# Attention scores from 64-row products of even and odd heads, in place of one product with a block-diagonal key operand

## The chip, the cores and the metric

The kernel runs on one NeuronCore of a Trainium2 chip. The metric is the device time of one execution in microseconds (us). TensorE (PE) multiplies, with its weight loads (PEld) listed apart; VectorE (DVE), ScalarE (ACT) and GpSimd (POOL) do the rest, and SyncE (SP) issues the DMAs. The kernel before takes 1671.57 us, the median of three runs from 1668.79 to 1672.21.

## The reference, cut to what matters

Attention over keys and values that are averaged in groups of 8, and then two feed-forward layers on its 4608 rows of 512. There are 8 batches of 8 heads, 576 queries, 72 pooled keys and 64 numbers per head.

```python
k_p = k.reshape(B, H, Sp, pool, D).mean(axis=3)
v_p = v.reshape(B, H, Sp, pool, D).mean(axis=3)
scores = scale * np.matmul(q, k_p.transpose(0, 1, 3, 2))
attn = np.exp(scores - scores.max(-1)); attn = attn / attn.sum(-1)
x = np.matmul(attn, v_p)               # then per token, heads side by side
h = x @ w_in;   x = (h * np.cos(h)) @ w_out
h = x @ w_in2;  out = (h * np.clip(h + 3, 0, 6) / 6) @ w_out2
```

The change touches `scores` alone.

## The kernel before, in words

**Attention.** Each batch is cut into five units of queries (`UNITS`): four of 128 and one of 64, so 40 units, 32 full and 8 short. A unit's queries lie as `qT[n]`, 128 rows by 4 pairs of heads by up to 128 queries: rows 0 to 63 hold the even head of a pair, rows 64 to 127 the odd one. The pooled keys of a batch (`kbd`) are a block-diagonal operand, 128 rows by 4 pairs by 144 columns: the even head's 72 keys stand in rows 0 to 63 of the first 72 columns, the odd head's in rows 64 to 127 of the other 72, and the rest is zero from two memsets at the start (line 718). One matmul of a pair, with `qT` as the stationary operand and `kbd` as the moving one, so gives the scores of both heads beside each other (line 515). Everything here is fp32.

`unit_s(n, half)` makes two such matmuls, pairs 0 and 1 or pairs 2 and 3, into one PSUM tile of 288 columns. DVE then takes the maxima (line 525) and subtracts them on the way to SBUF (line 528); for batch 0 ACT does the exponentials straight from PSUM (line 535). `unit_exp`, `unit_norm`, `unit_pt` (transposes on PE, lines 586 and 610) and `pv` (products with the values, line 628; for the first four batches the second product of each pair has 64 rows) follow. The transposes of a short unit have 64 rows as well.

The keys are pooled in three ways. For batch 0, DVE halves the raw keys and ACT writes `kbd` in two pieces (line 434). For batch 1, PE sums them against an identity matrix (line 440) and ACT writes two pieces (line 445). For batches 2 to 7, DVE does all of it, the last addition in two pieces of 64 rows (line 432).

**Order.** `front()` runs batch 0 alone, while the first weights arrive and are converted. From then on the attention is a generator that is advanced piece by piece between the feed-forward's matmuls (line 299, first product; line 341, second): after each gemm step so many pieces are taken that a goal is met (lines 940 to 950), and each `yield` in `attention()` ends a piece. In this mixed stretch all small pieces share two PSUM tiles (`ap_ps`); in `front()` scores take turns between an `ap_ps` and an `h` tile. The order in which instructions stand on each engine in the built program is then set by a scheduler, which may move a matmul back or forth among the others as its operands and tiles come free; PE itself runs its queue in order.

After the attention the rest of the feed-forward runs: gemm matmuls at lines 299, 341 and 998, nearly without pause.

Of the kernel before, what the change touches and what calls it, by code (L numbers as in the profile page):

```python
# [8 lines left out]
F32 = mybir.dt.float32  # L9
# [4 lines left out]
AF = mybir.ActivationFunctionType  # L14
ALU = mybir.AluOpType
# [14 lines left out]
def tile_kernel(ctx, tc, q, k, v, wi1, wo1, wi2, wo2, ident_d, mask_d, out):  # L30
    nc = tc.nc
    B, H, S, D = v.shape
    DM, NT = out.shape
    P = 128
    N = 512
    SP = S // POOL
    NP = H // 2
# [30 lines left out]
    UNITS = [(n0, min(P, S - n0)) for n0 in range(0, S, P)]  # L68
    NU = len(UNITS)
# [292 lines left out]
    ap = actx.enter_context(tc.tile_pool(name="ap", bufs=1))  # L362
# [4 lines left out]
    vm = {}  # L367
    vr = {"vrf": ap.tile([P, NP, 2, D], F32, tag="vrh", name="vrf")}
    raw, kp = {}, {}
    kbd = [ap.tile([P, NP, 2 * SP], F32, name=f"kbd{n}") for n in range(2)]  # L370
    NE = 4
    ebuf = [ap.tile([P, H * SP + P], F32, name=f"e{n}") for n in range(NE)]
    raw_k = ap.tile([P, POOL * NP * SP], F32, name="raw_k")
    raw_t = ap.tile([P, KC, POOL * D], F32, name="raw_v")
    qm, qT, pts = {}, {}, {}
# [6 lines left out]
    sums = {}  # L382
    FACTOR = 1.0 / (math.sqrt(D) * POOL)

    def piece(kind):
        turn = turns[kind] = turns.get(kind, -1) + 1
        if started:
            return ps_a.tile([P, N], F32, tag="ap", name="ap_ps", bufs=2)
        tag = SKIND[kind][turn % len(SKIND[kind])]
        if tag == "ap":  # L390
            return ps_a.tile([P, N], F32, tag="ap", name="ap_ps", bufs=2)
        if tag == "h":
            return ps_h.tile([P, N], F32, tag="h", name="h")
        return ps_y.tile([P, N], F32, tag=tag, name=tag)

    def load_kv(b, nm, step=POOL):
        if nm == "v":
            src = v[b].rearrange("h (s r) d -> (h s) (r d)", r=POOL)
            pairs = src.rearrange("(j x) e -> x j e", x=2 * SP)
            nc.sync.dma_start(out=raw_t[:, :NP, :], in_=pairs[:P])  # L400
            for half in range(2):
                o = half * NP * VR
                nc.sync.dma_start(
                    out=raw_t[o : o + NP * VR, NP, :],
                    in_=src.rearrange("(j x) e -> j x e", x=2 * SP)[:, P:],
                )
            return
        for c in range(0, POOL, step):
            cs = slice(c * NP * SP, (c + step) * NP * SP)
            nc.sync.dma_start(out=raw_k[:, cs], in_=k[b][:, cs])  # L410

    def load_q(n):
        b, i = divmod(n, NU)
        n0, w = UNITS[i]
        t = ap.tile([P, NP, P], F32, tag="qT", name="qT", bufs=4)
        nc.sync.dma_start(
            out=t[:, :, :w], in_=q[b, :, :, n0 : n0 + w].rearrange("j p n -> p j n")
        )
        qT[n] = t

    def pool_k(b, eng):
        t = raw_k
        w = POOL * NP * SP
        while w > (2 if b else 1) * NP * SP:
            w //= 2
            eng.tensor_tensor(out=t[:, :w], in0=t[:, :w], in1=t[:, w : 2 * w], op=ALU.add)
        t = t[:, : 2 * NP * SP].rearrange("p (r j x) -> p r j x", j=NP, x=SP)
        kb = kbd[b % 2]
        for e, p in enumerate((slice(0, D), slice(D, P))):
            to = kb[p, :, e * SP : (e + 1) * SP]  # L430
            if b:
                eng.tensor_tensor(out=to, in0=t[p, 0], in1=t[p, 1], op=ALU.add)
            else:
                nc.scalar.activation(out=to, in_=t[p, 0], func=AF.Copy, scale=FACTOR)

    def sum_k(b):

        ps = piece("k")[:, : NP * SP]
        for c in range(POOL):
            nc.tensor.matmul(  # L440
                ps, ident, raw_k[:, c * NP * SP : (c + 1) * NP * SP],
                start=(c == 0), stop=(c == POOL - 1),
            )
        for e, p in enumerate((slice(0, D), slice(D, P))):
            nc.scalar.activation(
                out=kbd[b % 2][p, :, e * SP : (e + 1) * SP],
                in_=ps[p].rearrange("p (j x) -> p j x", x=SP), func=AF.Copy, scale=FACTOR,
            )

    def sum_v(b):  # L450
        ps = piece("w")[:, : KC * D].rearrange("p (c d) -> p c d", d=D)
        for r in range(POOL):
            nc.tensor.matmul(
                ps, ident, raw_t[:, :, r * D : (r + 1) * D], start=(r == 0), stop=(r == POOL - 1)
            )
        kp[b, "v"] = ps
# [12 lines left out]
    def make_v(b):  # L469
# [27 lines left out]
        for x, src, rows in (("h", f(sp_h), P), ("l", sp_l, half)):  # L497
# [8 lines left out]
                op=ALU.mult,  # L506
            )

    def unit_s(n, half):
        b, i = divmod(n, NU)  # L510
        w = UNITS[i][1]
        ps = piece("s")
        t = qT[n]
        for j in range(2):
            nc.tensor.matmul(  # L515
                ps[:w, j * 2 * SP : (j + 1) * 2 * SP],
                t[:, 2 * half + j, :w],
                kbd[b % 2][:, 2 * half + j, :],
                start=True,
                stop=True,  # L520
            )
        s3 = ps[:w, : 4 * SP].rearrange("p (g s) -> p g s", s=SP)
        mx = ap.tile([P, 4, 8], F32, tag="mx", name="mx", bufs=2)[:, :, 0:1]
        early = b < EARLY
        nc.vector.tensor_reduce(out=mx[:w, :, 0], in_=s3, op=ALU.max, axis=AX.X, negate=early)  # L525
        e = ebuf[n % NE][:w, half * 4 * SP : (half + 1) * 4 * SP].rearrange("p (g s) -> p g s", s=SP)
        if not early:
            nc.vector.tensor_tensor(
                out=e, in0=s3, in1=mx[:w].to_broadcast([w, 4, SP]), op=ALU.subtract
            )  # L530
            return
        if half == 0:
            sums[n] = ap.tile([P, H, 4], F32, tag="sm", name="sm", bufs=3)[:, :, 0:1]
        for g in range(4):
            nc.scalar.activation(
                out=e[:, g], in_=s3[:, g], func=AF.Exp, bias=mx[:w, g], scale=1.0,
                accum_out=sums[n][:w, 4 * half + g],
            )

    def unit_exp(n):  # L540
# [164 lines left out]
    def front():  # L705

        load_kv(0, "k")
        w_fetch()
        load_q(0)
        nc.sync.dma_start(out=ident, in_=ident_d)  # L710
        load_q(1)
        load_kv(0, "v")
        nc.sync.dma_start(out=mask[:, : 2 + NP], in_=mask_d)
        load_q(2)
        load_q(3)
        w_fetch()
        for n in range(2):
            nc.vector.memset(kbd[n], 0.0)
        nc.gpsimd.memset(vr["vrf"], 0.0)
        pool_k(0, nc.vector)  # L720
        w_convert(3)

        def s(n):
            unit_s(n, 0)
            unit_s(n, 1)

        s(0)
        load_q(4)
        s(1)
        unit_norm(0)  # L730
        w_convert(1)
        s(2)
        unit_norm(1)
        sum_v(0)
        unit_pt(0)
        s(3)
        make_v(0)
        load_kv(1, "k")
        w_ops(1)
        unit_pt(1)  # L740
        unit_pt_rest(0, 0)
        unit_norm(2)
        s(4)
        for j in range(NP):
            pv(0, 0, j)
        unit_norm(3)
        unit_pt(2)
        w_ops(1)
        unit_norm(4)
        unit_pt(3)  # L750
        unit_pt_rest(0, 2)
        unit_pt(4)
        (sum_k(1) if SUMMED > 1 else pool_k(1, nc.vector))
        load_kv(1, "v")
        load_q(5)
        load_q(6)
        load_q(7)
        w_convert(3)
        for j in range(NP):
            pv(0, 1, j)  # L760
        done.append(0)
        started.append(0)

    steps = []
    for bl in range(NB):
        n = NAL[bl]
        steps += [(0, (0, bl), bl, fc, fc == 0, fc == n - 1) for fc in range(n)]
    SA = len(steps)
    for bl in range(NB):
        n = NAL[bl]  # L770
# [10 lines left out]
    def w_fetch():  # L781
        nonlocal fetched
        if fetched < len(wjobs) and fetched < converted + 2:
            fetch_weights(*wjobs[fetched][:3])
            fetched += 1
# [4 lines left out]
    def w_ops(n):  # L790
        while running and n:
            running.pop(0)()
            n -= 1
            if not running:
                whole.add(wjobs[converted - 1][:3])
                w_fetch()
# [9 lines left out]
    def w_convert(n=3):  # L806
        nonlocal converted
        m, fc, hf, home = wjobs[converted]
        converted += 1
        running.extend(convert_weights(m, fc, hf))  # L810
        w_ops(n)
# [83 lines left out]
    for slot in range(2 * (T + LAG) + 4):  # L895
        s, odd = divmod(slot, 2)
        for fn in after.pop(slot, ()):
            fn()
        if not odd and s < T:
# [9 lines left out]
            if key[0] == 1 and fc == NF - 5:  # L909
                for c in range(NC):  # L910
                    t = ypl.tile([P, N], F32, tag="yv", name="yv", bufs=4)
                    nc.sync.dma_start(
                        out=t, in_=yp_d[c * P : (c + 1) * P, bl * N : (bl + 1) * N]
# [25 lines left out]
        if live:  # L939
            key = steps[s][1]  # L940
            i = sum(1 for x in steps[:s] if x[1] == key)
# [163 lines left out]
    for pb, (t0, w) in enumerate(PAIRS):  # L1105
# [3 lines left out]
        for g in range(4):  # L1109
# [17 lines left out]
            for n in range(7):  # L1127
# [4 lines left out]
                x = EARLY.get((g, n)) if pb == 0 else n if g == 3 else None  # L1132
# [15 lines left out]
    for step, pb in enumerate(ORDER2):  # L1148
        t0, w = PAIRS[pb]
# [75 lines left out]
```

## Time and profile before

| | |
|---|---|
| median of 3 runs | 1671.57 us |
| profiled execution | 1672.67 us |
| its span | 1670.9 us |
| PE / PEld busy | 1639.7 / 1348.0 us |
| DVE / ACT / POOL busy | 1108.9 / 891.6 / 311.9 us |

The profile is of one execution. Its span is counted from the first to the last instruction; what lies around it makes the execution's own time 1.8 us longer. A fp32 matmul appears in it as two matmul instructions with two weight loads; fp32r (the gemms) as one of each. Records of PE overlap, since a matmul's fill and drain run beside its neighbours, so the pace of PE is read from the distance between starts and not from the durations.

### The profile page before, as it was taken

Reading aid. Unit: us, or ns where it says so; the run is one execution under the profiler, and the core shown is the slowest. Engines: PE = TensorE matmul, PEld = TensorE weight load, DVE = VectorE, ACT = ScalarE, POOL = GpSimd, SP = SyncE. Lnnn points to the kernel's source line nnn. Section 1 sums busy time; section 2 is a strip of 40 time slices with the busy share of each in tenths; the row PEclk is TensorE's granted clock in tenths of the full one; section 3 lists DMA queues with packets and bytes.
Section 4 is the critical chain, followed back from the end, with each engine's and each line's share of the span. In section 5 each row is a group of like instructions: output and inputs, shape, how many; then the busy total and the mean of one; then the engine's idle time right before and its main releaser. Section 6 shows DMA issues by size and latency. Waiting matters only on the chain.

```text
span 1670.9 us, 21107 instructions
## 1 busy us (share of the span) xinstructions
PE 1639.7 (98%) x7674; PEld 1348.0 (81%) x7674; DVE 1108.9 (66%) x1536; ACT 891.6 (53%) x1320; POOL 311.9 (19%) x248
## 2 busy tenths in 40 slices
PE   6999999999999999999999999999999999999999
PEld 4656778888888888888888898888878888888889
DVE  5798666665767788878786445445364676768665
ACT  6667677776556554555555334444353444444444
POOL 3365343322223110111114001020120000000000
PEclk8999999999999999999999999999999999999999
DMA  7665351223333476666664483242439954335130
GB/s 241 205 217 195 115 182 51 92 89 124 114 114 119 143 246 198 209 213 202 187 189 154 152 290 141 111 164 114 177 130 336 341 185 168 130 123 170 58 118 34
DMA packets 154183, 273.03 MB, mean 163 GB/s; under 512 B 15712, under 2 KB 79328, under 8 KB 153056
## 3 DMA queue, kind: packets, MB, share of 16 engines
q1 hardware_dynamic: 154080, 271.70, 48.0%
q8 instruction: 60, 0.98, 0.2%
q14 instruction: 43, 0.35, 0.1%
HBM read 166.79 MB, written 104.86 MB: 163 GB/s over the span
## 4 chain that ended last, share of the span: by engine, by line
PE 93%; DVE 3%; DMA 2%; ACT 1%; issue 1%; POOL 1%; SPq 0%; POOLq 0%; DVEq 0%; ACTq 0%
PE bank L998 41%; PE h L299 22%; PE y L341 22%; PE ap_ps L628 3%; PE ap_ps L515 2%; PE ap_ps L586 1%; PE y L628 1%; DMA xr<-x_d 0%; DMA qT<-in_q_dram 0%; DMA st<-in_moe_w_out_dram 0%; POOL xl L277 0%; DVE a L132 0%; DVE mx L525 0%; PE y L440 0%; POOL e L557 0%
## 5 line engine op out<-in xcount | busy, mean ns | idle before, releaser
L998 PE MATMUL bank<-wa,wb 128*128 128x512 f32 (+1 forms) x1368 | 287.7, 358 | 0.0
L998 PEld LDWEIGHTS bank<-wa,wb 128*128 128x128 f32 x1368 | 231.2, 189 | 37.7
L299 PE MATMUL h<-xh,wb 128*128 128x512 f32 x648 | 211.2, 389 | 0.0
L341 PE MATMUL y<-gh,wb 128*128 128x512 f32 x648 | 210.8, 389 | 0.0
L860 ACT ACTIVATE wa<-wu 128x1024 fp32r<-128x1024 f32 (+1 forms) x130 | 127.3, 980 | 141.5 <-PE bank L998 121.4
L998 PE MATMUL bank<-wu,wb 128*128 128x512 f32 (+1 forms) x792 | 198.4, 386 | 0.0
L299 PE MATMUL h<-xh,wa 128*128 128x512 f32 x504 | 172.8, 402 | 2.5 <-ACT xh L276 2.5
L998 PEld LDWEIGHTS bank<-wu,wb 128*128 128x128 f32 x792 | 148.8, 188 | 29.9
L311 DVE SCALAR_TENSOR_TENSOR g<-h,t 128x512 f32<-128x512 f32 x144 | 99.0, 687 | 108.5 <-ACT t L306 108.1
L341 PE MATMUL y<-gh,wa 128*128 128x512 f32 x504 | 170.9, 399 | 0.0
L277 POOL TENSOR_TENSOR xl<-xr,xh 128x512 fp32r<-128x512 f32 x68 | 94.2, 1402 | 323.8 <-ACT xh L276 322.3
L306 ACT ACTIVATE t<-h 128x512 int32<-128x512 f32 x144 | 85.3, 592 | 124.3 <-PE h L299 123.8
L314 ACT ACTIVATE g<-g,bias_c 128x512 f32<-128x512 f32 x144 | 104.3, 724 | 79.7 <-DVE g L311 78.9
L299 PEld LDWEIGHTS h<-xh,wb 128*128 128x128 f32 x648 | 121.7, 188 | 25.2
L341 PEld LDWEIGHTS y<-gh,wb 128*128 128x128 f32 x648 | 121.6, 188 | 25.2
L321 ACT ACTIVATE gh<-g 128x512 fp32r<-128x512 f32 x144 | 90.4, 628 | 71.9 <-DVE g L318 71.6
L861 DVE TENSOR_TENSOR wa<-wu,wa 128x1024 fp32r<-128x1024 f32 (+1 forms) x80 | 89.4, 1122 | 57.2 <-ACT wa L860 57.1
L299 PE MATMUL h<-xl,wb 128*128 128x512 f32 x324 | 126.2, 389 | 0.0
L341 PE MATMUL y<-gl,wb 128*128 128x512 f32 x324 | 126.1, 389 | 0.0
L318 DVE TENSOR_TENSOR g<-h,g 128x512 f32<-128x512 f32 x144 | 98.6, 684 | 32.4 <-ACT g L314 31.6
L998 PE MATMUL bank<-wa,wa 128*128 128x512 f32 (+1 forms) x552 | 117.4, 359 | 0.0
L299 PEld LDWEIGHTS h<-xh,wa 128*128 128x128 f32 x504 | 94.6, 189 | 23.9 <-ACT xh L276 2.8
(177 smaller groups left out, 2854.9 us busy)
## 6 DMA issues: line engine op xcount, KB each, us to landing
g_d<-wu SPq DMA_DIRECT2D x64, 512.0 KB
wu<-g_d SPq DMA_DIRECT2D x56, 512.0 KB
wb<-s_d SPq DMA_DIRECT2D x36, 512.0 KB
xr<-x_d SPq DMA_DIRECT2D x68, 256.0 KB
s_d<-wa SPq DMA_DIRECT2D x32, 512.0 KB
s_d<-wa SPq DMA_DIRECT2D x32, 384.0 KB
raw_k<-in_k_dram SPq DMA_DIRECT2D x8, 1152.0 KB
yp_d<-ys SPq DMA_DIRECT2D x36, 256.0 KB
```

Source lines behind the costliest of these rows:

```text
L277: nc.gpsimd.tensor_tensor(out=xl, in0=t, in1=f(xh), op=ALU.subtract)
L299: nc.tensor.matmul(h, a[:, cs], z, start=(n == 0), stop=(n == 3 * NC - 1))
L306: nc.scalar.activation(out=t, in_=hs[s], func=AF.Copy, bias=0.25, scale=INV_2PI)
L311: mark[s] = nc.vector.scalar_tensor_tensor(out=g, in0=hs[s], scalar=INV_2PI, in1=t, op0=ALU.mult, op1=ALU.subtract)
L314: nc.scalar.activation(out=g, in_=g, func=AF.Sin, scale=TWO_PI, bias=bias_c[:, 1:2])
L318: nc.vector.tensor_tensor(out=g, in0=hs[s], in1=g, op=ALU.mult)
L321: nc.scalar.activation(out=gh, in_=g, func=AF.Copy)
L341: nc.tensor.matmul(y[c], a, z, start=(first and n == 0), stop=(last and n == 2))
L628: nc.tensor.matmul(ps[:, :w], a[:, j].rearrange("p e d -> p (e d)"), z[:, :w], start=(n == 0), stop=(n == len(prods) - 1),)
L860: nc.scalar.activation(out=hi, in_=src, func=AF.Copy)
L861: el.tensor_tensor(out=lo, in0=src, in1=f(hi), op=ALU.subtract)
L998: nc.tensor.matmul(bank[:, e, :wide], w[:, j, h, e], z[:, j], start=start and j == 0 and x == 0, stop=stop and j == 1 and x == 2, skip_gro ...
```

## The change

Even and odd heads get products of their own. The pooled keys lie as `pooled_k`, 128 rows by 4 pairs by 72 columns, without zeros; a matmul takes the 64 rows of one head from `qT` and `pooled_k` and gives its 72 columns of scores. `unit_mm(n)` makes all eight of a unit, even and odd in turn, into two PSUM tiles, when `unit_s(n, 0)` is called; `unit_s(n, 1)` makes none and reads the second tile. A half is now "all even heads" or "all odd heads", so the results are written in blocks of 72 at every second place. The writes of pooled keys, two pieces of 64 rows each before, become one of 128 rows, and the two memsets go.

```diff
-    kbd = [ap.tile([P, NP, 2 * SP], F32, name=f"kbd{n}") for n in range(2)]
+    pooled_k = [ap.tile([P, NP, SP], F32, name=f"pk{n}") for n in range(2)]
...
-        for e, p in enumerate((slice(0, D), slice(D, P))):
-            to = kb[p, :, e * SP : (e + 1) * SP]
-            if b:
-                eng.tensor_tensor(out=to, in0=t[p, 0], in1=t[p, 1], op=ALU.add)
-            else:
-                nc.scalar.activation(out=to, in_=t[p, 0], func=AF.Copy, scale=FACTOR)
+        w = NP * SP
+        to = pooled_k[b % 2].rearrange("p j x -> p (j x)")
+        if b:
+            eng.tensor_tensor(out=to, in0=t[:, :w], in1=t[:, w : 2 * w], op=ALU.add)
+        else:
+            nc.scalar.activation(out=to, in_=t[:, :w], func=AF.Copy, scale=FACTOR)
...
+    def unit_mm(n):
+        b, i = divmod(n, NU)
+        w = UNITS[i][1]
+        ps = [piece("s") for _ in range(2)]
+        for j in range(NP):
+            for half, rows in enumerate((slice(0, D), slice(D, P))):
+                nc.tensor.matmul(
+                    ps[half][:w, j * SP : (j + 1) * SP],
+                    qT[n][rows, j, :w],
+                    pooled_k[b % 2][rows, j, :],
+                    start=True,
+                    stop=True,
+                )
+        scores[n] = ps
...
     def unit_s(n, half):
-        ps = piece("s")
-        t = qT[n]
-        for j in range(2):
-            nc.tensor.matmul(
-                ps[:w, j * 2 * SP : (j + 1) * 2 * SP],
-                t[:, 2 * half + j, :w],
-                kbd[b % 2][:, 2 * half + j, :],
...
+        if half == 0:
+            unit_mm(n)
+        ps = scores[n][half]
...
-        e = ebuf[n % NE][:w, half * 4 * SP : (half + 1) * 4 * SP].rearrange("p (g s) -> p g s", s=SP)
+        e = ebuf[n % NE][:w, : H * SP].rearrange("p (g t s) -> p t g s", t=2, s=SP)[:, half]
...
-        for n in range(2):
-            nc.vector.memset(kbd[n], 0.0)
```

The order on PE shows what the scheduler makes of it. In the rows, `qT_389` and the like are the queries of one unit, `ap_ps_520` one PSUM tile, `kbd1`/`pk1` the keys; a matmul is one row here, though it runs as two instructions. First, on PE, the third unit of batch 1, before:

```order
L515 MATMUL ap_ps_520<-kbd1_102,qT_389 128x144 x2
L299 MATMUL h_735<-xh_319,wa5_656 128x512
L299 MATMUL h_735<-xh_329,wa4_655 128x512
L299 MATMUL h_735<-xl_330,wa4_655 128x512
L299 MATMUL h_735<-xh_329,wa5_656 128x512
L515 MATMUL ap_ps_526<-kbd1_102,qT_389 128x144 x2
```

and the same unit now (line 515 has become 514):

```order
L514 MATMUL ap_ps_544<-pk1_102,qT_405 128x72 x4
L299 MATMUL h_778<-xh_346,wa4_690 128x512
L299 MATMUL h_778<-xl_347,wa4_690 128x512
L299 MATMUL h_778<-xh_346,wa5_691 128x512
L341 MATMUL y0_846<-gh_471,wa0_132 128x512
L514 MATMUL ap_ps_545<-pk1_102,qT_405 128x72 x4
```

Each half is four matmuls in place of two, and gemm matmuls still stand between the halves: even and odd heads don't alternate here. Second, on PE, the fourth unit of batch 2, before:

```order
L586 MATMUL ap_ps_922<-ident_98,e2_105 128x128 x4
L515 MATMUL ap_ps_940<-kbd0_101,qT_698 128x144 x2
L341 MATMUL y0_803<-gl_975,wa8_860 128x512
L341 MATMUL y0_803<-gh_974,wa9_861 128x512
L341 MATMUL y1_804<-gh_974,wa8_860 128x512
L341 MATMUL y1_804<-gl_975,wa8_860 128x512
L341 MATMUL y1_804<-gh_974,wa9_861 128x512
L341 MATMUL y2_805<-gh_974,wa8_860 128x512
L341 MATMUL y2_805<-gl_975,wa8_860 128x512
L341 MATMUL y2_805<-gh_974,wa9_861 128x512
L341 MATMUL y3_806<-gh_974,wa8_860 128x512
L515 MATMUL ap_ps_946<-kbd0_101,qT_698 128x144 x2
```

and now:

```order
L341 MATMUL y1_847<-gh_1024,wa9_904 128x512
L514 MATMUL ap_ps_986<-pk0_101,qT_737 128x72
L514 MATMUL ap_ps_987<-pk0_101,qT_737 128x72
L514 MATMUL ap_ps_986<-pk0_101,qT_737 128x72
L514 MATMUL ap_ps_987<-pk0_101,qT_737 128x72
L514 MATMUL ap_ps_986<-pk0_101,qT_737 128x72
L514 MATMUL ap_ps_987<-pk0_101,qT_737 128x72
L514 MATMUL ap_ps_986<-pk0_101,qT_737 128x72
L514 MATMUL ap_ps_987<-pk0_101,qT_737 128x72
L341 MATMUL y2_848<-gh_1024,wa8_903 128x512
```

Here the two halves have come together, and even (`ap_ps_986`) and odd (`ap_ps_987`) alternate between the gemm matmuls.

## Rows read from the trace of the kernel before

**Rows 1.** The page: its first line, and one engine's busy us, share, instructions.

```profile
span 1670.9 us, 21107 instructions
...
PE 1639.7 (98%) x7674; PEld 1348.0 (81%) x7674; DVE 1108.9 (66%) x1536; ACT 891.6 (53%) x1320; POOL 311.9 (19%) x248
```

**Rows 2.** Windows: length us, busy us by engine (PE first), granted clock, DMA share, GB/s.

```profile
0.00:40.00 40.00, 25.21 (x98) 18.37 (x98) 22.42 (x49) 24.25 (x106) 13.76 (x20) 0.85 0.78 244
40.00:400.00 360.00, 348.52 (x1676) 268.31 (x1676) 254.97 (x466) 258.68 (x419) 150.64 (x137) 0.98 0.43 138
400.00:1671.00 1271.00, 1265.99 (x5903) 1061.32 (x5902) 831.55 (x1022) 608.63 (x798) 147.49 (x91) 1.00 0.49 168
```

**Rows 3.** Line 515: count, shortest/median/longest ns, first and last start us; who waited.

```profile
L515 PEld LDWEIGHTS ap_ps<-kbd,qT x300: 132/189/338, 9.8 to 386.1; 128*128 128x128 f32 x120, 128*64 128x64 f32 x30
L515 PE MATMUL ap_ps<-kbd,qT x300: 283/286/610, 9.8 to 386.2; 128*128 128x144 f32 x120, 128*64 128x144 f32 x30
...
  DVE mx L525: 43.6, 26
```

**Rows 4.** Waits of PE, 40 to 400 us: us in total, times, longest us.

```profile
PE ap_ps L586 <- DVE e L528: 3.3, 2, 3.0
...
PE ap_ps L515 <- DVE ptl L593: 1.8, 2, 1.3
```

**Rows 5.** Timeline of PE around 270 us: start us, length us, instruction, shapes, count.

```profile
270.07 0.39 PE L341 MATMUL y<-gh,wa 128*128 128x512 f32 x1
270.30 1.14 PE L515 MATMUL ap_ps<-kbd,qT 128*128 128x144 f32 x8
...
271.52 0.40 PE L299 MATMUL h<-xl,wa 128*128 128x512 f32 x1
```

**Rows 6.** Timeline of PE around 201 us.

```profile
201.12 0.39 PE L341 MATMUL y<-gh,wa 128*128 128x512 f32 x1
201.44 0.52 PE L586 MATMUL ap_ps<-ident,e 64*128 64x64 f32 x5
201.89 0.50 PE L299 MATMUL h<-xh,wa 128*128 128x512 f32 x1
202.23 0.39 PE L299 MATMUL h<-xl,wa 128*128 128x512 f32 x1
```

**Rows 7.** Timeline of PE from 205 us.

```profile
205.21 0.70 PE L628 MATMUL ap_ps<-pf,vmf 128*128 128x320 f32 x2
205.84 0.80 PE L628 MATMUL ap_ps<-pf,vrf 64*128 64x320 f32 x2
206.58 0.81 PE L628 MATMUL ap_ps<-pf,vmf 128*128 128x320 f32 x2
207.31 0.80 PE L628 MATMUL ap_ps<-pf,vrf 64*128 64x320 f32 x2
```

**Rows 8.** Timeline of weight loads from 205 us, same columns.

```profile
205.84 0.29 PEld L628 LDWEIGHTS ap_ps<-pf,vrf 64*128 64x128 f32 x2 [0.44 <-issue]
206.57 0.30 PEld L628 LDWEIGHTS ap_ps<-pf,vmf 128*128 128x128 f32 x2 [0.44 <-issue]
...
209.85 0.19 PEld L341 LDWEIGHTS y<-gl,wa 128*128 128x128 f32 x1
```

**Rows 9.** Timeline of PE around 335 us.

```profile
334.62 1.20 PE L515 MATMUL ap_ps<-kbd,qT 128*64 128x144 f32 x8
...
336.08 0.62 PE L341 MATMUL y<-gh,wa 128*128 128x512 f32 x2
```

**Rows 10.** Chain that ended last, first 62 us: start us, us, what.

```profile
9.65 6.82 DMA st<-in_moe_w_out_dram
...
19.25 0.96 PE ap_ps L515 x4
20.21 0.86 PE h L515 x4
```

**Rows 11.** Windows: one shorter stretch.

```profile
100.00:150.00 50.00, 46.68 (x202) 31.14 (x201) 44.54 (x73) 34.15 (x59) 27.87 (x25) 0.97 0.67 220
```

More of the change, by code (lines that the diff above doesn't have):

```diff
@@ L426, in pool_k @@
             eng.tensor_tensor(out=t[:, :w], in0=t[:, :w], in1=t[:, w : 2 * w], op=ALU.add)
-        t = t[:, : 2 * NP * SP].rearrange("p (r j x) -> p r j x", j=NP, x=SP)
-        kb = kbd[b % 2]
-        for e, p in enumerate((slice(0, D), slice(D, P))):
-            to = kb[p, :, e * SP : (e + 1) * SP]
-            if b:
-                eng.tensor_tensor(out=to, in0=t[p, 0], in1=t[p, 1], op=ALU.add)
-            else:
-                nc.scalar.activation(out=to, in_=t[p, 0], func=AF.Copy, scale=FACTOR)
+        w = NP * SP
[4 more added lines that the diff above has]
+            nc.scalar.activation(out=to, in_=t[:, :w], func=AF.Copy, scale=FACTOR)
     def sum_k(b):
@@ L443, in sum_k @@
             )
[L444 to L448, printed above, removed]
+        nc.scalar.activation(
+            out=pooled_k[b % 2].rearrange("p j x -> p (j x)"), in_=ps, func=AF.Copy, scale=FACTOR
+        )
     def sum_v(b):
@@ L507, in make_v @@
             )
+    scores = {}
+    def unit_mm(n):
[10 more added lines that the diff above has]
+                    stop=True,
+                )
+        scores[n] = ps
     def unit_s(n, half):
@@ L511, in unit_s @@
         w = UNITS[i][1]
-        ps = piece("s")
-        t = qT[n]
-        for j in range(2):
-            nc.tensor.matmul(
-                ps[:w, j * 2 * SP : (j + 1) * 2 * SP],
-                t[:, 2 * half + j, :w],
-                kbd[b % 2][:, 2 * half + j, :],
-                start=True,
-                stop=True,
-            )
+        if half == 0:
+            unit_mm(n)
+        ps = scores[n][half]
         s3 = ps[:w, : 4 * SP].rearrange("p (g s) -> p g s", s=SP)
@@ L536, in unit_s @@
                 out=e[:, g], in_=s3[:, g], func=AF.Exp, bias=mx[:w, g], scale=1.0,
-                accum_out=sums[n][:w, 4 * half + g],
+                accum_out=sums[n][:w, 2 * g + half],
             )
```

## The prediction

> **What bounds the kernel now.** I read the page first: TensorE's matmuls cover 98% of the span of 1670.9 us [rows 1]. Then the table by stretches, to see whether that share also holds where the change lies. All score matmuls (line 515) start between 9.8 and 386.2 us [rows 3], so three stretches matter [rows 2]. In the first 40 us PE is busy for 25.2 us: it waits there. From 40 to 400 us it is busy for 348.5 of 360.0 us, while DVE has 255.0 and ACT 258.7. After 400 us it is full (1265.99 of 1271). So from 40 us on a microsecond added to PE's queue is a microsecond added to the end, except for what falls into its 11.5 us of idle time; and 28 full units (128 queries) and 7 short ones (64 queries) of the 40 lie there. The list of PE's waits there is short and scattered, 3.3 us on a DVE subtraction as the largest [rows 4]. PE binds by its own pace, and the question is what one score matmul takes in that queue.
>
> **What a score matmul costs now.** PE's records overlap, so I take differences of starts, not durations. A fp32 matmul appears as two instructions, each with its own weight load. Eight of them, both halves of a unit, begin at 270.30 and the second gemm matmul after them at 271.52: 1.22 us, of which 0.23 is one gemm matmul (270.07 to 270.30), so 0.99 for eight, 0.12 each [rows 5]. A half unit (four) takes 0.49. No load shows: it runs beside the matmul before it.
>
> **What is removed and added on PE.** A half unit now has four matmuls of 64 rows x 72 columns, eight instructions in place of four. The columns streamed are the same: 8 x 0.06 = 0.48. If streaming were all, PE would gain and lose nothing. Three other things come in.
>
> First, the array's shape. The rows of lines 628 and 586 show what a 64-row matmul between 128-row ones costs. The last gemm matmul before the 64-row transposes starts at 201.12 and they at 201.44, 0.32 in place of 0.23: 0.09 for going in. Going out, the first gemm matmul takes until 202.23, 0.34 in place of 0.23: 0.11 more, since its load starts only after the change of shape [rows 6]. At line 628, where both shapes alternate, a 128-row pair that follows a gemm takes 0.63 (205.21 to 205.84), one between two 64-row pairs 0.73 (206.58 to 207.31): the 0.10 is the exposed load; and 0.63 against two passes of 0.27 leaves 0.09 for the change itself [rows 7] (0.27 is 0.12 scaled from 144 to 320 columns). So a change costs 0.09, and the first load behind it, 0.11 at 128 columns, isn't hidden.
>
> Second, the pace of loads. Right behind each change two loads stand back to back, so their pace can be read: two take 0.29 to 0.30 in all, one 0.19, so the second begins 0.10 to 0.11 after the first, with 64 rows (0.29) as with 128 rows (0.30) [rows 8]. I take 0.108. Now a matmul streams for 0.12 and covers it; a 72-column one streams for 0.06 and does not. PE then goes by loads: 8 x 0.108 = 0.86 for a half unit.
>
> The Trainium skill, "TensorE: Matmul & The Clock Gate", section "LDWEIGHTS (loading the stationary operand)", says that a load's time goes by the columns loaded and not by the rows, about 107 ns for 128 columns; rows 8 agree (64 rows no cheaper), which speaks against the change and against the third rival below.
>
> Third, the short units. Their loads have 64 columns; the shortest load of the line is 132 ns and the median 189 [rows 3], so they save 0.06 of the 0.108, some 0.05 is left, and the 0.06 of streaming covers it. They already run in a shape of their own (128x64) and already pay the changes: 334.62 to 336.08 is 1.46, less 0.23 is 1.23, in place of 0.99 [rows 9]. For them I add nothing.
>
> Sum for one full half unit alone between gemms: 0.09 in, 0.86 loads, 0.06 for the last pass, 0.09 out, 0.11 exposed gemm load = 1.21; less 0.49 makes +0.72.
>
> **How many stand alone.** The source writes the two halves in turn, but the order of the built program has them apart where the second PSUM tile is free later (the first piece of order, from batch 1, shows it; in the second, from batch 2, they alternate). Counted over the order behind the first gemm: of 28 full units 17 have their halves apart (34 groups), 7 alternate strictly, 3 partly, 1 has them in a row.
> - 34 x 0.72 = 24.5.
> - 6 of all these groups stand next to 64-row work (five behind line 628's second product, one ahead of the short unit's transposes) and save a change on their side and the one that stood there: 0.40 each, -2.4.
> - 11 units together, 16 loads one after the other: 0.09 + 1.73 + 0.06 + 0.09 + 0.11 = 2.08, less 0.98: +1.10 each, 12.1.
> Together +34.2. Whether loads for the upper and the lower 64 rows run beside each other no row here shows, since no 64-row work at the upper rows stands in this trace; one after the other is what rows 8 show and what I take. Side by side is a rival.
>
> **The other edits.** In the first 40 us the five units of batch 0 alternate strictly. One of them is on the chain there, 0.96 + 0.86 us [rows 10], with the granted clock at 0.85 over these 40 us [rows 2]; by loads alone 16 would take 1.7 at full clock and 3.5 at half, so +0 to +1.6, and later units may be covered by line 628's wait. I take +1. Gone are the two memsets, at the start while the first loads are under way, and one of the two ACT copies of the first keys: the first score starts earlier, but the chain runs over the load of the weights until 16.46 us [rows 10]: 0. The key sums of batches 2 to 7 take six DVE instructions in place of twelve, those of batch 1 one ACT copy in place of two, and DVE idles for 105 us of the stretch [rows 2]: 0, at best the 5.1 us that PE waits there for DVE in two groups [rows 4]. DVE and ACT write blocks of 72 at twice the distance: as many elements, 0. A score half now ends 0.7 later for DVE, which waits 43.6 us for line 515 as it is [rows 3] and has that slack: 0, at worst 0.7 for each of the few groups on which a transpose hangs next, some 5.
>
> Part of the added PE time falls into the 11.5 us of waits: while PE is slower, DVE, ACT and GpSimd catch up. I take 3, some of the 5.1 that hang on DVE [rows 4]; bounds 0 and 11.5.
>
> Total: 34.2 + 1 - 3 = +32.2. Against the profiled execution (1672.67 us, 1.8 of it around the span) that is 1704.9; that execution is 1.1 above the median of 1671.57, so 1704.
>
> **Rivals.**
> 1. The two row halves work side by side. The Trainium skill, "TensorEngine Tiling (Array Packing)", section "Tiling Modes", says that tiles load and multiply independently and in parallel. As a mechanism here: the 7 strictly alternating units take 8 loads' time in place of 16 (-0.86 each, -6), the 3 mixed ones some 0.3 less each: +25, about 1697. The 17 separated units gain nothing. No row speaks against it. 18%.
> 2. Other engines bound the stretch after all and the whole 11.5 us of idle PE time takes up added work: +24, about 1695. For it: PE is busy for only 46.68 of the 50 us behind 100 us, with DVE at 44.54 [rows 11]; against it: the waits are short and few, and PE's share of the whole stretch is 97%. 6%.
> 3. Loads of 64 rows are half as long, hidden under 0.06: a half unit costs 0.09 + 0.48 + 0.05 + 0.09 + 0.11 - 0.49 = +0.33, 34 of them 11.2, the 11 joint units +0.35 each, less 2.4: 12.7, and with +1 - 3 about 1682. Against it: rows 8. 8%.
> 4. It gets faster. That needs loads hidden, both row halves side by side and no price for the change of shape; then the 11 joint units take 0.5 for 0.98, -5.3, the rest nothing: about 1666. Rows 6 and 7 show the price, three times over; it decides only where the price of lines 586 and 628 doesn't hold for line 514, though its shape of 64 rows x 128 columns is that of line 628. 4%.
> 5. The half-clock spells grow. From 100 to 150 us the granted clock is 0.97 [rows 11], a spell at the lower level that costs 3% of 50 us, 1.5; a PE queue with more holes could have several more. Or PE waits for the second PSUM tile, now claimed by the first half's code, with gemm matmuls queued behind it. Four to six such events: +8, 1712. 9%.
>
> **Numbers.** 55% for 1704 with its own range 1698 to 1710. The range reaches from the third rival to a little beyond the fifth: 1681 to 1716. A measurement of this kernel can tell about 0.2%, 3.3 us, from no change. Faster by more than that: rival 4, 4%. Within: 2%, where several rivals come together. Slower: 94%.
>
> **What would show it.** Score matmuls of full units starting 0.10 to 0.11 apart, and not 0.06; a gap of 0.09 ahead of and behind each group; some 80 more changes of shape in the whole trace; PE's idle time between 40 and 400 us smaller than 11.5; the gemm phases after it as long as before (1271 us), only shifted. In alternating units, pairs of starts almost at once would speak for rival 1. Wrong would be the forecast if line 514's starts are 0.06 apart, or if the stretch from 40 to 400 us doesn't grow.

## The result, and the profile after

The changed kernel takes 1690.13 us, the median of 4 runs (1688.56 to 1695.89); the kernel before took 1671.45 us in runs beside it. The ratio is 1.0112, 95% interval 1.0094 to 1.0129: slower by 18.7 us. Forecast were +32, with a range from +9 to +44; the narrower range that had 55%, 1698 to 1710, was missed. The profiled execution has a span of 1688.5 us, 17.6 more than before.

The page of the changed kernel (answers to [rows 1]):

```profile
span 1688.5 us, 21728 instructions
...
PE 1658.4 (98%) x7994; PEld 1360.2 (81%) x7994; DVE 1105.1 (65%) x1528; ACT 894.2 (53%) x1320; POOL 312.2 (18%) x248
```

Its stretches, in the columns of [rows 2]:

```profile
0.00:40.00 40.00, 23.70 (x132) 16.55 (x133) 19.93 (x45) 22.03 (x100) 12.46 (x19) 0.91 0.73 226
40.00:400.00 360.00, 351.37 (x1860) 268.13 (x1859) 242.60 (x438) 249.23 (x398) 150.03 (x135) 1.00 0.42 136
400.00:1688.00 1288.00, 1283.31 (x6007) 1075.47 (x6004) 842.57 (x1046) 622.97 (x822) 149.70 (x94) 1.00 0.49 167
```

PE is still the engine that binds, a little fuller than before (351.4 of 360 in place of 348.5), and the granted clock in the mixed stretch is 1.00 where it was 0.98. The last score matmul starts 19 us later than before (405.5, in [rows 3] 386.2), and from there to the end of the span it is 1283.0 us, before 1284.7:

```profile
L514 PE MATMUL ap_ps<-pk,qT x600: 222/272/487, 9.4 to 405.5; 64*128 64x72 f32 x120, 64*64 64x72 f32 x30
...
  DVE mx L532: 43.8, 35
```

So the loss lies in the attention, and the gemms behind it are only shifted. The number of changes of shape on PE behind the first gemm matmul rises from 86 to 164, counted over the matmul records of both traces. Now one half unit alone between gemm matmuls, by the timeline of PE (columns of [rows 5]):

```profile
62.51 0.62 PE L299 MATMUL h<-xh,wa 128*128 128x512 f32 x2
63.07 1.11 PE L514 MATMUL ap_ps<-pk,qT 64*128 64x72 f32 x8
64.11 0.50 PE L299 MATMUL h<-xl,wa 128*128 128x512 f32 x1
64.45 0.40 PE L299 MATMUL h<-xh,wa 128*128 128x512 f32 x1
```

From 62.51 two gemm matmuls should take 0.46 and take 0.56, so some 0.09 for going in. From 63.07 to 64.45 it is 1.38; less one gemm matmul (0.23) that leaves 1.15. Together that is 1.24, against 0.49 before: +0.75, forecast +0.72. All but the first of the starts within the group are 0.112 apart (0.06, the time of a 72-column pass, would be seen if loads were hidden). Beside 64-row work the way in is free, as forecast:

```profile
220.30 0.80 PE L635 MATMUL ap_ps<-pf,vrf 64*128 64x320 f32 x2
220.94 1.00 PE L514 MATMUL ap_ps<-pk,qT 64*128 64x72 f32 x8
221.88 0.50 PE L341 MATMUL y<-gh,wa 128*128 128x512 f32 x1
222.21 0.40 PE L341 MATMUL y<-gl,wa 128*128 128x512 f32 x1
```

(1.27 from 220.94 to 222.21 in place of 1.38.) And a unit whose halves alternate:

```profile
254.07 0.39 PE L299 MATMUL h<-xh,wa 128*128 128x512 f32 x1
254.38 1.11 PE L514 MATMUL ap_ps<-pk,qT 64*128 64x72 f32 x16
255.43 0.50 PE L341 MATMUL y<-gh,wa 128*128 128x512 f32 x1
255.77 0.39 PE L341 MATMUL y<-gl,wa 128*128 128x512 f32 x1
```

Sixteen instructions take from 254.38 to 255.77, which is 1.39, as much as eight above. One after the other they would take 2.25 (the eight more at 0.108 each). That is the first rival: starts come in pairs 0.007 us apart.

PE's waits from 40 to 400 us (columns of [rows 4]) have changed place and become fewer:

```profile
PE h L299 <- POOL xl L277: 4.3, 2, 2.8
PE ap_ps L593 <- POOL spl L492: 1.4, 1, 1.4
```

**An account of the 17.6 us.** From each whole trace I took the distance from the first gemm matmul (line 299) to the last matmul, less PE's idle time in it, less what spells at the lower of the clock's two levels cost (for each matmul begun in such a spell: the distance to the next start, less idle time, less the median distance of the same pair of shapes at the full level). The rest is PE's own work:

| kernel | first gemm at | idle | clock | work | median time | ratio to before |
|---|---|---|---|---|---|---|
| before | 51.08 | 12.57 | 2.86 | 1600.3 | 1671.45 | |
| changed | 49.26 | 10.01 | 1.41 | 1623.7 | 1690.13 | 1.0112 |
| apart | 52.27 | 8.37 | 6.27 | 1625.8 | 1698.63 | 1.0159 |
| narrow128 | 46.93 | 10.94 | 8.43 | 1620.6 | 1692.47 | 1.0123 |
| joint | 49.15 | 8.01 | 12.82 | 1618.8 | 1693.03 | 1.0124 |
| late | 50.59 | 7.70 | 1.38 | 1617.0 | 1682.54 | 1.0057 |
| joint_late | 53.17 | 13.40 | 14.06 | 1610.7 | 1690.99 | 1.0122 |
| same_rows | 54.58 | 6.91 | 12.49 | 1629.5 | 1704.73 | 1.0193 |
| joint_late_pv | 49.12 | 15.50 | 6.16 | 1606.5 | 1678.88 | 1.0045 |
| pv128 | 47.78 | 18.47 | 2.99 | 1593.0 | 1667.89 | 0.9973 |

All times are in us; the other rows are the experiments below, each profiled once. Matching the pairs of shapes in other ways moves clock and work by up to 1.4, so differences of work below that say nothing. Changed less before: work +23.4, start -1.8, idle -2.6, clock -1.4, together +17.6.

### The profile page after: what moved, and what is told of

Same layout as the page of the kernel before. It is cut to its first block, busy times and chain, and to the rows that moved or that the text cites. A ratio compares the mean times of both kernels' runs of the same rounds, so it can differ in the third digit from the quotient of the medians.

```text
span 1688.5 us, 21728 instructions
## 1 busy us (share of the span) xinstructions
PE 1658.4 (98%) x7994; PEld 1360.2 (81%) x7994; DVE 1105.1 (65%) x1528; ACT 894.2 (53%) x1320; POOL 312.2 (18%) x248
## 4 chain that ended last, share of the span: by engine, by line
PE 92%; DVE 3%; DMA 2%; ACT 1%; POOL 1%; issue 1%; SPq 0%; POOLq 0%; ACTq 0%; DVEq 0%
PE bank L1003 41%; PE y L341 22%; PE h L299 22%; PE ap_ps L514 3%; PE ap_ps L635 3%; PE ap_ps L593 1%; PE y L635 1%; DMA st<-in_moe_w_out_dram 0%; DMA qT<-in_q_dram 0%; POOL xl L277 0%; DVE sm L561 0%; POOL wa L866 0%; DMA raw_v<-in_v_dram 0%; PE ap_ps L449 0%; DMA st<-y_d 0%
## 5 line engine op out<-in xcount | busy, mean ns | idle before, releaser
L1121 ACT ACTIVATE wu<-bank,bias_c 128x1024 f32<-128x1024 f32 (+1 forms) x60 | 61.7, 1030 | 94.3 <-PE bank L1003 94.2
```

## The experiments

The theory to be tested: each group of 64-row score matmuls pays for the change of the array's shape, and goes by the pace of weight loads, 0.112, instead of that of columns; where upper and lower rows alternate they run side by side and the second half is nearly free. Rivals: the shape alone is the cost; loads run one after the other; the loss comes from waits.

**Loads without a change of shape (narrow128).** The kernel before, each score matmul cut in two, all with 128 rows:

```diff
-            nc.tensor.matmul(
-                ps[:w, j * 2 * SP : (j + 1) * 2 * SP],
-                t[:, 2 * half + j, :w],
-                kbd[b % 2][:, 2 * half + j, :],
+            for e in range(2):
+                nc.tensor.matmul(
+                    ps[:w, (2 * j + e) * SP : (2 * j + e + 1) * SP],
+                    t[:, 2 * half + j, :w],
+                    kbd[b % 2][:, 2 * half + j, e * SP : (e + 1) * SP],
```

> The kernel before with its block-diagonal keys, but each matmul of 144 columns cut into two of 72, all with 128 rows: no change of array shape, only the pace of loads. Theory: a half alone takes 8 x 0.112 = 0.90 in place of 0.49, a whole unit 1.79 in place of 0.98; 26 x 0.41 + 15 x 0.81 = 23 us at most, less some waits that it fills: 1685 to 1694, ratio 1.008 to 1.014. Rival (the change of shape is the whole cost and loads stay hidden): the kernel before, 1671.

Measured 1692.47 us, ratio 1.0123 (1.0108 to 1.0138). PE's work grows by 20.3 us over the kernel before (23 forecast). Its timeline:

```profile
253.86 0.39 PE L299 MATMUL h<-xh,wa 128*128 128x512 f32 x1
254.09 1.90 PE L516 MATMUL ap_ps<-kbd,qT 128*128 128x72 f32 x16
255.79 0.48 PE L341 MATMUL y<-gh,wa 128*128 128x512 f32 x1
256.11 0.39 PE L341 MATMUL y<-gl,wa 128*128 128x512 f32 x1
```

No gap of 0.09 ahead (254.09 less 253.86 is 0.23), and 2.02 from 254.09 to 256.11, less 0.23 is 1.79 for sixteen: 0.112 each. The same columns in twice as many matmuls take 0.80 more per unit, for loads alone. The time follows the work because the rest cancels (start -4.2, idle -1.6, clock +5.6). The rival that the shape is the whole cost falls.

**Both halves on the same rows (same_rows), against joint_late.** joint_late issues all score matmuls of a unit in its second piece, odd head first and the others queued behind it:

```diff
-                unit_s(n, 0)
                 yield
+                unit_s(n, 0)
                 unit_s(n, 1)
...
+        heads = [(j, half) for j in range(NP) for half in (1, 0)]
+        lead = one(*heads[0])
+        with tc.issue_after(lead.ins):
+            for j, half in heads[1:]:
+                one(j, half)
```

> All score matmuls of a unit are issued in its second piece, odd and even in turn, so more units have both halves together: 20 of 28 full units behind the first gemm in place of 11. Theory (a change of array shape and loads that a 72-column pass doesn't cover, paid per group, halved where upper and lower rows alternate): from the changed kernel's trace a group alone adds 0.75 us, a strictly alternating unit 0.26, a mixed one 0.53. That makes 17.9 in place of 27.3 us, so 9 us under the changed kernel: 1681, ratio to the kernel before 1.0055. Rival (the loss comes from later halves and waits of DVE and PE): a half that is issued later still makes it no faster, 1690 or more.

same_rows takes `rows = slice(0, D)` for both:

> As joint_late, in the same order, but both halves take the lower 64 rows (the even heads' queries and keys stand in for the odd heads', whose scores are left out): nothing can run side by side. Theory (upper and lower rows load and multiply side by side): a strictly alternating unit goes from 1.05 to 1.94 us, a mixed one from 1.32 to 1.94, a short one from 0.65 to 1.1; 13, 6 and 6 of them: PE's work behind the first gemm, idle time and the cost of the lower clock taken off, grows by 18 us over joint_late's 1610.7. Rival (they run one after the other anyway, and starts recorded 7 ns apart mean nothing): the same 1611.

Measured for same_rows 1704.73 us (ratio 1.0193, 1.0169 to 1.0216), PE's work 1629.5, 18.8 us over joint_late. A unit in it, and one that alternates in joint_late:

```profile
210.24 0.39 PE L299 MATMUL h<-xh,wa 128*128 128x512 f32 x1
210.56 2.00 PE L516 MATMUL ap_ps<-pk,qT 64*128 64x72 f32 x16
212.49 0.50 PE L341 MATMUL y<-gh,wa 128*128 128x512 f32 x1
212.83 0.39 PE L341 MATMUL y<-gl,wa 128*128 128x512 f32 x1
```

```profile
210.56 0.39 PE L299 MATMUL h<-xh,wa 128*128 128x512 f32 x1
210.87 1.11 PE L516 MATMUL ap_ps<-pk,qT 64*128 64x72 f32 x16
211.92 0.50 PE L341 MATMUL y<-gh,wa 128*128 128x512 f32 x1
212.26 0.39 PE L341 MATMUL y<-gl,wa 128*128 128x512 f32 x1
```

It takes 1.93 against 1.05 up to the next gemm's load, with the same count and shape: only the rows differ. That the two halves run side by side is shown.

joint_late itself measured 1690.99 us (ratio 1.0122, 1.0102 to 1.0142), and 1681 was expected. Its PE work did fall, by 13.0 us against the changed kernel (9 expected). The rest took it back: clock 12.7 us more, idle 3.4 more, start 3.9 later (its profiled execution, at 1697.22, is the longest of its four, with a clock of 0.986; the others have 0.989 to 0.991). The windows of joint_late and of late (below) from 100 to 145 us, clock third from the end:

```profile
100.00:125.00 25.00, 23.09 (x83) 14.18 (x81) 19.27 (x33) 12.60 (x22) 10.85 (x9) 0.67 0.61 209
125.00:145.00 20.00, 17.36 (x71) 12.01 (x70) 12.25 (x24) 10.13 (x18) 11.31 (x10) 0.73 0.65 208
```

```profile
100.00:125.00 25.00, 22.66 (x128) 15.13 (x126) 22.63 (x37) 16.31 (x30) 14.05 (x12) 1.00 0.75 241
125.00:145.00 20.00, 19.26 (x98) 13.53 (x98) 17.52 (x31) 13.21 (x22) 10.48 (x10) 1.00 0.68 226
```

PE looks as busy in both, but runs 154 matmuls in joint_late against 226: at the lower level each takes longer. One wait of PE just ahead of the first spell is on record, ahead of the row

```profile
107.19 0.81 PE L642 MATMUL ap_ps<-pf,vmf 128*128 128x320 f32 x2 [1.73 <-ACT pf L604]
```

**late and joint: the two edits of joint_late, each alone.**

> The changed kernel with all score matmuls of a unit in its second piece, without the order odd-first that joint_late adds: 17 full units with both halves together in place of 11. Theory: 7 us less PE work than the changed kernel (1616.7 in place of 1623.7 behind the first gemm); the time follows only if idle time and clock stay, 1683. Rival (pieces issued later leave PE holes behind 100 us, in which the granted clock falls, and these give the gain back): 1690 again, with a longer spell at the lower clock between 100 and 145 us.

> The changed kernel with the odd-first order alone, pieces where they were: 14 full units together in place of 11. Theory: 2 us less PE work than the changed kernel, about 1688 with its clock; 1690 to 1695 if the spells at the lower clock come back. Rival (order within a unit matters in itself): outside 1684 to 1697.

late: 1682.54 us, ratio 1.0057 (1.0037 to 1.0078), work 1617.0: the forecast to 0.5 us in both. joint: 1693.03 us, ratio 1.0124 (1.0099 to 1.0148), work 1618.8 (4.9 less than the changed kernel, 2 forecast), but 12.8 us of clock cost from a spell at the lower level between 103 and 130 us. So more halves together cost less PE work in each of the three, and the time follows only where the clock stays up. The rival on late, that pieces issued later bring the lower clock, falls. The odd-first order is in joint and joint_late, but it isn't what all long spells have in common: apart (17 us from 114) and narrow128 (twice 10 us, from 110 and from 130) have them without it. What brings them isn't settled.

**No unit alternates in the program (apart).** Each half issues its own four matmuls:

```diff
-        ps = [piece("s") for _ in range(2)]
+        rows = slice(half * D, (half + 1) * D)
+        ps = piece("s")
         for j in range(NP):
-            for half, rows in enumerate((slice(0, D), slice(D, P))):
...
-        if half == 0:
-            unit_mm(n)
-        ps = scores[n][half]
+        unit_mm(n, half)
+        ps = scores[n, half]
```

> Each half issues its own four 64-row matmuls, so no unit alternates: 13 full units with the halves apart and 15 with one half after the other. Theory: 26 groups at 0.75 and 15 units at 1.04, less 4 neighbours of 64-row work at 0.4, makes 33.4 in place of 27.3: 1696, ratio 1.015. Rival that the row halves gain nothing from alternating: as the changed kernel, 1690. Rival of waits (PSUM tiles claimed too early by the first half's code cost time): faster than the changed kernel, under 1687.

Measured 1698.63 us, ratio 1.0159 (1.0140 to 1.0178). The time agrees, but not for the reason given: PE's work is only 2.1 us over the changed kernel's, 6 expected, and 4.9 us are clock. A unit with one half behind the other shows why:

```profile
64.67 0.39 PE L299 MATMUL h<-xh,wa 128*128 128x512 f32 x1
64.99 1.62 PE L514 MATMUL ap_ps<-pk,qT 64*128 64x72 f32 x16
66.53 0.50 PE L299 MATMUL h<-xh,wa 128*128 128x512 f32 x1
66.87 0.39 PE L299 MATMUL h<-xl,wa 128*128 128x512 f32 x1
```

From 64.99 to 66.53 it is 1.54, between the 1.05 of alternating halves and the 1.93 on the same rows. In the built program the eight lower instructions stand ahead of the eight upper ones, but in the trace the first upper one starts 0.006 us behind the fifth lower one, and the lower half's last, which carries the semaphore update that ends it, is the eleventh to start. So PE does not keep to the order of its queue across the two row halves, and halves one behind the other overlap in part: 15 such units cost 0.3 us less each than expected, 4.4 in all, which is the missing work. The experiment so doesn't switch the overlap off; same_rows does. The rival of waits falls all the same: idle time is lower than in the changed kernel by 1.6 and the time is higher.

**The price of the shape, taken out of the kernel before (pv128).**

```diff
-            prods = [(vm["vmf"], ph[:, j]), (vr["vrf"][:half], ph[:half, NP])]
+            prods = [(vm["vmf"], ph[:, j]), (vr["vrf"], ph[:, NP])]
```

> The kernel before, but the second value product of batches 0 to 3 takes all 128 rows (the lower 64 of its value operand are zero) in place of 64, so that it keeps the array's shape: 34 changes of shape behind the first gemm in place of 86. Theory: 52 changes at 0.20 us are 10 us: 1661, ratio 0.994. Rival (the gaps at line 628 come from something else than the number of rows): no change, 1671.

Measured 1667.89 us, ratio 0.9973 (0.9963 to 0.9984): 4 us faster than the kernel before, where 10 were expected. Its pairs at line 628, to be read against [rows 7]:

```profile
198.99 0.70 PE L628 MATMUL ap_ps<-pf,vmf 128*128 128x320 f32 x2
199.53 0.70 PE L628 MATMUL ap_ps<-pf,vrf 128*128 128x320 f32 x2
200.07 0.70 PE L628 MATMUL ap_ps<-pf,vmf 128*128 128x320 f32 x2
200.61 0.70 PE L628 MATMUL ap_ps<-pf,vrf 128*128 128x320 f32 x2
```

0.54 a pair in place of 0.73: the change of shape and the exposed load are gone, as the theory has it. Over all groups of line 628 behind the first gemm matmul the price of the changes falls by 9.7, near the 10 expected. PE's work as a whole falls by 7.3: part of the gain turned into waits, and as a matmul's record runs 0.16 us past the next start (0.39 against 0.23), that much of each wait counts as work. PE waits 30 times in place of 19 there, which by this estimate is 1.8 of the 2.4 missing. Idle time grows by 5.9, from 12.57 to 18.47: PE now waits for GpSimd and DVE in the mixed stretch. The start comes 3.3 earlier, but the kernel before has a spell at the lower level there that pv128 has not, from 31.1 to 44.7 us, so it isn't shown to be a gain of the edit. PE's waits from 40 to 420 us:

```profile
PE ap_ps L586 <- DVE e L528: 3.3, 1, 3.3
PE h L299 <- POOL xl L277: 2.9, 4, 1.0
PE ap_ps L515 <- issue: 2.5, 1, 2.5
```

**Both (joint_late_pv).** joint_late with the line of pv128.

> joint_late with the 128-row second value product of pv128: 44 changes of shape fewer behind the first gemm. Theory: 44 x 0.20 = 8.8 us less PE work, 1602 in place of 1610.7, as much as the kernel before has (1600.3). The time, with 13 us idle and up to 14 us of clock cost as in joint_late, 1678 to 1683; at the kernel before's clock 1671. Rival (as in pv128 the gain turns into waits for DVE and GpSimd): 1686 or more, PE idle over 17 us.

Measured 1678.88 us, ratio 1.0045 (1.0028 to 1.0062); work 1606.5, 4.2 less than joint_late and not 8.8, idle 15.5. That the time is as expected is luck: the work that didn't go is made up by a clock cost of 6.2 in place of up to 14. Where the other 4.6 us of work went was not followed up. It is the best of the 64-row kernels and still behind the kernel before.

## Why the prediction was right or wrong

**Right: the direction, and each price per group.** PE binds; 64-row score matmuls between 128-row gemms pay 0.09 on the way in, go by loads at 0.11, and pay 0.09 and an exposed load on the way out. +0.75 a half unit was measured for +0.72, and narrow128 shows the load part of it by itself. The third rival (half loads for 64 rows) is dead: 0.112 with 64 rows and with 128.

**Wrong: "one after the other is what rows 8 show and what I take".** Rows 8 show two loads for the same rows. Loads for upper and lower rows overlap, and so do their matmuls (same_rows); rival 1, given 18%, is what happened. The 11 units with both halves together were put at +1.10 each, 12.1. In the trace six of the 7 alternating ones cost 1.25 against 0.99, +0.26 each, the seventh 1.42, and the 3 mixed ones 1.52: some 8 us less. Short units, put at 0, gain 0.3 to 0.5 where they alternate (4 of 7), 1.6 in all. PE's work so came out at +23.4 in place of +34.2; about 1 us of that difference I did not follow up.

**Outrun by the clock: the first 40 us.** Put at +1, bounds 0 and 1.6; measured -1.8 up to the first gemm matmul. Up to the first value product behind batch 0's scores the changed kernel is 1.6 us later; the four rows are of before, changed, before, changed:

```profile
29.41 0.70 PE L628 MATMUL y<-pf,vmf 128*128 128x256 f32 x2 [2.45 <-ACT pf L590]
31.00 0.70 PE L635 MATMUL y<-pf,vmf 128*128 128x256 f32 x2 [3.17 <-ACT pf L597]
42.16 5.31 PE L440 MATMUL y<-raw_k,ident 128*128 128x288 f32 x16
42.30 4.04 PE L438 MATMUL y<-raw_k,ident 128*128 128x288 f32 x16
```

From there to the first gemm matmul it is 21.67 us before and 18.26 in the changed kernel, 3.4 less, and that is the clock: it is at its lower level from 31.1 to 44.7 us before and from 31.8 to 38.7 in the changed kernel, 6.8 us less at half speed. The key sum for batch 1 (sixteen instructions behind 42 us) shows it, with 3.9 in place of 5.2. Nothing on record ties that to the edit, and narrow128 and pv128 have no such spell ahead of the first gemm matmul. Nor is the +1.6 the price of the scores: in pv128, whose scores are those of the kernel before, the same product starts at 30.70. So the +1 was neither confirmed nor refuted.

**Right in size: the waits.** Idle time fell by 2.6, put at 3. The two groups that hang on DVE in [rows 4], 5.1 us, came down to 0.9, as forecast; PE's waits for GpSimd (line 277) grew from 0.4 to 4.3.

**Not in the sum: the clock.** It gave 1.4 us back behind the first gemm matmul and 3.4 ahead of it, and in the experiments it came to between -1.5 and +11 against the kernel before. Rival 5 had it only as a loss. These 4.8 us are luck: nothing in the prediction or in the runs ties them to the edit.

So of 32.2 forecast: -10.8 from work, -2.8 at the start (the clock's 3.4 among them), +0.4 idle, -1.4 clock, which is the 17.6 measured. The change does remove the multiplications by zero, but those were free: a 128-row matmul with zeros costs the same columns, and a 144-column pass hid its load.

## What to carry to other kernels

On a PE queue that binds, count three things for a small matmul: its columns, the load it must hide (0.112 us for 128 columns here, where a 144-column fp32 pass took 0.122, so by estimate a pass under about 130 columns doesn't hide it), and whether its shape differs from its neighbours' (about 0.2 us each way with the exposed load). Two 64-row products come cheap only where upper and lower rows stand close together in the built order (a full unit cost 1.25 alternating, 1.74 one half behind the other, twice 1.24 apart, and 0.99 in the block-diagonal form), so read that order and not the source; zero rows that keep the shape may be cheaper, as pv128 shows. And look at idle time and granted clock beside the work: of 13 us less PE work in joint_late nothing reached the time.

## What the runs showed that I had not expected

Matmuls on upper and lower rows with separate PSUM tiles start 0.007 us apart and cost a pair what one costs (1.05 for sixteen, against 1.93 on the same rows).

The text ahead of the prediction says that PE runs its queue in order. Between the two row halves it doesn't: in apart upper-row matmuls start ahead of lower-row ones that stand before them.

The share of granted clock differs more between some programs than between runs of one: 0.997 or 0.998 in all four runs of late, 0.986 to 0.991 in all four of joint_late, whose sources differ only in the order within a unit. Within the changed kernel three runs at 0.997 took 1688.56 to 1690.28 and one at 0.993 took 1695.89. The long spells lie between 100 and 145 us, where DVE is nearly as loaded as PE [rows 11]. An idle PE alone doesn't bring them: from 115 to 125 us the changed kernel's PE is busy for 6.92 of 10 us and the granted clock is 1.00. What makes the clock fall there in one program and not in another stays open.
